# Converting float64 weights to float32 on the chip: the sign as whole words by PoolE, the low bits over it by ScalarE

## The chip, the cores and the metric

The kernel runs on one core of one Trainium2 chip. The core has five engines with queues of their own: TensorE (PE in the profile, with its weight loads as PEld), VectorE (DVE), ScalarE (ACT), PoolE (POOL) and SyncE (SP), which here issues the transfers. Each engine takes its instructions strictly in the order of its queue, and an instruction waits for those of other engines that it depends on. The metric is the device time of one execution in microseconds.

## The reference

Three layers stand one behind the other: a chunked state space layer ("attention"), a leaky MLP, and a mixture of experts with one expert per token.

```python
# x (4, 8, 768, 32), a (4, 8, 768), B and C (4, 8, 768, 16), float32, in chunks of 32
M = (C_c @ B_c.T) * exp(cum_i - cum_j) * causal
y = M @ x_c + (C_c @ state) * exp(cum)
state = exp(sum la) * state + sum_j B_j x_j exp(cum_last - cum_j)
# then rows of 256, 3072 tokens
h = x @ w_in                          # w_in (256, 2048), float64
x = (maximum(0.01 * h, h) @ w_out).astype(float32)   # w_out (2048, 256), float64
# then per token one of 8 experts, chosen by argmax of x @ w_gate + modality_bias
out[mask] = gate_w * (maximum(x[mask] @ w1[e], 0) @ w2[e])
```

The inputs w_in and w_out come as float64, since they are float32 arrays divided by a float64 number. [...]

## The kernel before

The tokens go through in blocks of 512. For a block, four attention chunks of 128 tokens are computed (attn_tr or attn_split and attn_stack, attn_cb, attn_p3), and their result xh, xl (the float32 value as a rounded part and a rest, both of type float32r) is multiplied by w_in in 16 column tiles (mm1, which makes h, then sa, gg, gh, gl) and by w_out (mm2, which sums into y). Six matmuls per pair of tiles do the work of one product of float32 accuracy: each weight, too, is a rounded part (wih, woh) and a rest (wil, wol).

The weights are converted in the first part of the program, 16 tiles of 128x512 numbers, eight of w_in (split_win, two per column quarter) and eight of w_out (split_wout). Each lies in SBUF as raw (four 16-bit words per number) and goes through to_f32, in five steps on three engines, and then two of split:

- ACT writes hb from the high word of the float64 (as a float32 it has 8 exponent bits, the scale of 2^-112 moves the exponent into place).
- POOL writes the two 16-bit halves of the word lb: into the lower half a number worked out from the second 16-bit word of raw (times LOW plus LOW0, the "low" operation), into the upper half the sign (the fourth 16-bit word of raw is_ge 32768, times 32768, the "sign" operation).
- DVE shifts hb left by 3 and ors lb over it.
- ACT rounds hb into wih or woh (split, s.copy), and POOL subtracts that from hb into wil or wol (split, eng is POOL for all tiles, by Q['sg']).

hb and lb have two buffers each (the tags "hb" and "lb" of pool ap_): hb of a tile can be written only when the subtraction of the tile two before is done, and lb only when DVE's or of the tile two before is done. POOL also masks e, the decay of an attention chunk (attn_mask, the affine select), after its transfer from cumd has landed. The first four tiles (buffers 292, 350, 547 and 555) are converted in the prologue, the other twelve while block 0 is multiplied: mm1 of column tiles 4 to 7 needs the tiles 605 and 631, and so on in order.

A scheduler that simulates a timeline sets the order of the instructions on each engine from the order in which the program lists them. Where the table Q['pin'] names a function, the operations of the engines that it gives stay in the program's order. keep (the matmuls wps of zeros) is there to keep TensorE busy.

Of the kernel before, what the change touches and what calls it, by code (L numbers as in the profile page):

```python
# [13 lines left out]
AF = mybir.ActivationFunctionType  # L14
ALU = mybir.AluOpType
# [5 lines left out]
LOW, LOW0 = 0.9 * 2.0 ** -13, 0.2995  # L21
# [68 lines left out]
def kernel(  # L90
# [70 lines left out]
    v, s, g, t_ = Pinned(nc.vector, "v"), Pinned(nc.scalar, "s"), Pinned(nc.gpsimd, "g"), Pinned(nc.tensor, "t")  # L161
# [375 lines left out]
    def to_f32(raw, q):  # L537

        w = raw.bitcast(I32).rearrange("p (f w) -> p f w", w=2)
        hb = ap_.tile([P, 512], F32, tag="hb", name="hb")  # L540
        lb = ap_.tile([P, 512], I32, tag="lb", name="lb")
        s.activation(out=hb, in_=w[:, :, 1].bitcast(F32), func=AF.Copy, scale=2.0 ** -112)
        w4 = raw.bitcast(U16).rearrange("p (f w) -> p f w", w=4)
        l2 = lb.bitcast(U16).rearrange("p (f w) -> p f w", w=2)
        g.tensor_scalar(out=l2[:, :, 0], in0=w4[:, :, 1], scalar1=LOW, scalar2=LOW0, op0=ALU.mult, op1=ALU.add)
        g.tensor_scalar(out=l2[:, :, 1], in0=w4[:, :, 3], scalar1=32768.0, scalar2=32768.0, op0=ALU.is_ge, op1=ALU.mult)
        hi = hb.bitcast(I32)
        v.scalar_tensor_tensor(out=hi, in0=hi, scalar=3, in1=lb, op0=ALU.logical_shift_left, op1=ALU.bitwise_or)
        return hb
# [13 lines left out]
    def split_win(k, kk):  # L563
        r = raws["i", k]
        os = slice(k * 512, (k + 1) * 512)
        f = to_f32(r[:, kk, :], kk) if W64 else r[:, kk, :]
        split(f, wih[:, kk, os], wil[:, kk, os], g if kk in Q["sg"] else v)
# [6 lines left out]
    def split_wout(k, q):  # L574
        r = raws["o", k]
        os = slice(k * 4 + 2 * q, k * 4 + 2 * q + 2)
        f = r[:, 2 * q:2 * q + 2, :].rearrange("p a d -> p (a d)")
        f = to_f32(f, q) if W64 else f
        split(
            f, woh[:, os, :].rearrange("p a d -> p (a d)"), wol[:, os, :].rearrange("p a d -> p (a d)"), g if q in Q["sg"] else v  # L580
        )
# [485 lines left out]
```

## Time and profile before

| | us |
|---|---|
| runs, median of 3 (lowest, highest) | 571.35 (570.81, 574.28) |
| the profiled execution, own time | 569.56 |
| its span, first to last instruction | 567.7 |
| busy in the span: PE, DVE, ACT, POOL | 529.3, 355.7, 332.7, 213.7 |
| mean granted TensorE clock | 0.962 |

The profiled execution has 1.86 us around its span and lies 1.79 us below the median of the runs. In the names of the trace buffer numbers are left out; in the orders of the program they stand, so lb_695 and hb_694 are the same tile's buffers. Every instruction has line 154, that of a helper that records them, so instructions are told apart by the names of their tiles: the line tells nothing. A bracket at the end of a timeline row is the idle time of the engine before it, and what released it.

### The profile page before, as it was taken

Reading aid. Unit: us, or ns where it says so; the run is one execution under the profiler, and the core shown is the slowest. Engines: PE = TensorE matmul, PEld = TensorE weight load, DVE = VectorE, ACT = ScalarE, POOL = GpSimd, SP = SyncE. Lnnn points to the kernel's source line nnn. Section 1 sums busy time; section 2 is a strip of 40 time slices with the busy share of each in tenths; the row PEclk is TensorE's granted clock in tenths of the full one; section 3 lists DMA queues with packets and bytes.
Section 4 is the critical chain, followed back from the end, with each engine's and each line's share of the span. In section 5 each row is a group of like instructions: output and inputs, shape, how many; then the busy total and the mean of one; then the engine's idle time right before and its main releaser. Section 6 shows DMA issues by size and latency. Waiting matters only on the chain.

```text
span 567.7 us, 9531 instructions
## 1 busy us (share of the span) xinstructions
PE 529.3 (93%) x3414; PEld 427.5 (75%) x3417; DVE 355.7 (63%) x707; ACT 332.7 (59%) x694; POOL 213.7 (38%) x184
## 2 busy tenths in 40 slices
PE   7888899699999999999999999999989999999990
PEld 3345465377876778878777787788879999999990
DVE  5646385787757676778576866656486566455630
ACT  4326566667676657775775675464436666566630
POOL 5838999810300120011200202431063445665431
PEclk9978888999999999999999999999979999999996
DMA  7897442232133315421322084412054765777400
GB/s 141 178 211 177 124 161 51 57 61 57 9 90 75 79 12 94 103 57 13 71 72 47 2 149 134 149 38 75 1 167 136 242 201 188 235 236 239 129 20 23
DMA packets 128440, 61.13 MB, mean 108 GB/s; under 512 B 84641, under 2 KB 120642, under 8 KB 128386
## 3 DMA queue, kind: packets, MB, share of 16 engines
q1 hardware_dynamic: 125314, 54.03, 37.6%
q0 software_dynamic: 3072, 6.42, 3.4%
q8 instruction: 29, 0.48, 0.4%
q14 instruction: 25, 0.20, 0.1%
HBM read 53.74 MB, written 6.69 MB: 106 GB/s over the span
## 4 chain that ended last, share of the span: by engine, by line
PE 75%; POOL 7%; issue 6%; DVE 5%; ACT 3%; DMA 1%; SPq 1%; POOLq 0%; DVEq 0%
PE h L154 21%; PE y L154 20%; PE hp L154 11%; PE o L154 10%; PE psy L154 5%; POOL lb L154 3%; PE cb L154 2%; POOL e L154 1%; PE yr L154 1%; PE pb L154 1%; PE xps L154 1%; PE pc L154 1%; DVE gl L154 1%; PE lp L154 1%; DVE hb L154 1%
## 5 line engine op out<-in xcount | busy, mean ns | idle before, releaser
L154 DVE TENSOR_TENSOR gl<-gg,gh 128x512 fp32r<-128x512 f32 x96 | 71.4, 744 | 44.6 <-ACT gh L154 44.0
L154 ACT CAST gh<-gg 128x512 fp32r<-128x512 f32 x96 | 59.5, 620 | 67.9 <-DVE gg L154 67.8
L154 PE MATMUL h<-xh,wih 128*128 128x512 f32 x192 | 79.0, 416 | 5.5 <-DVE gg L154 5.1
L154 DVE TENSOR_TENSOR gg<-sa,h 128x512 f32<-128x512 f32 x96 | 65.5, 682 | 23.2 <-ACT sa L154 22.8
L154 POOL TENSOR_SCALAR_AFFINE_SELECT e<-e 128x1024 f32<-128x1024 f32 (+1 forms) x28 | 28.9, 1044 | 134.0 <-DMA e<-cumd 70.2
L154 PE MATMUL h<-xh,wil 128*128 128x512 f32 x192 | 77.0, 403 | 2.0 <-POOL wil L154 1.9
L154 PE MATMUL h<-xl,wih 128*128 128x512 f32 x192 | 77.0, 401 | 1.4 <-DVE xl L154 1.4
L154 PE MATMUL y<-gl,woh 128*128 128x512 f32 x192 | 77.3, 406 | 0.7 <-DVE gl L154 0.7
L154 PE MATMUL y<-gh,wol 128*128 128x512 f32 x192 | 75.2, 397 | 1.2 <-POOL wol L154 1.2
L154 PE MATMUL hp<-x2h,w1s 128*128 128x256 f32 x384 | 73.9, 288 | 0.0
L154 ACT ACTIVATE sa<-h 128x512 f32<-128x512 f32 x96 | 57.3, 597 | 22.5 <-PE h L154 22.2
L154 PE MATMUL o<-w2s,hh 128*128 128x256 f32 x384 | 69.2, 285 | 0.0
L154 DVE SCALAR_TENSOR_TENSOR hl<-hp,hh 128x512 fp32r<-128x512 f32 x48 | 33.0, 691 | 54.9 <-ACT hh L154 54.8
L154 PE MATMUL y<-gh,woh 128*128 128x512 f32 x192 | 65.9, 407 | 0.0
L154 POOL TENSOR_TENSOR w2s<-r,w2s 128x1024 fp32r<-128x1024 f32 x12 | 33.5, 2792 | 79.8 <-ACT w2s L154 53.8
L154 PEld LDWEIGHTS hp<-x2h,w1s 128*128 128x128 f32 x384 | 62.9, 197 | 0.6
L154 PEld LDWEIGHTS o<-w2s,hh 128*128 128x128 f32 x384 | 58.3, 191 | 0.4 <-issue 0.4
L154 POOL TENSOR_SCALAR lb<-raw 128x512 uint16<-128x512 uint16 x32 | 51.3, 1602 | 14.5 <-issue 11.7
L154 PE MATMUL hp<-x2l,w1s 128*128 128x256 f32 x192 | 54.6, 289 | 0.0
L154 ACT ACTIVATE hh<-hp 128x512 fp32r<-128x512 f32 x48 | 28.5, 597 | 41.9 <-PE hp L154 41.9
L154 PE MATMUL o<-w2s,hl 128*128 128x256 f32 x192 | 51.1, 283 | 0.0
L154 ACT ACTIVATE e<-e,ncum 128x128 f32<-128x128 f32 x160 | 50.9, 392 | 0.0
(205 smaller groups left out, 997.8 us busy)
## 6 DMA issues: line engine op xcount, KB each, us to landing
r<-in_moe_w_dram SPq DMA_DIRECT2D x48, 512.0 KB, 4.5
e<-cumd SPq DMA_DIRECT2D x20, 512.0 KB, 4.7
raw<-in_moe_w_in_dram SPq DMA_DIRECT2D x4, 1024.0 KB, 6.7
raw<-in_moe_w_out_dram SPq DMA_DIRECT2D x4, 1024.0 KB, 5.8
yx<-ysb SPq DMA_DIRECT2D x6, 528.0 KB, 3.6
xt<-in_x_dram SPq DMA_DIRECT2D x24, 128.0 KB, 4.3
ct<-in_C_dram SPq DMA_DIRECT2D x24, 64.0 KB, 3.1
bt<-in_B_dram SPq DMA_DIRECT2D x24, 64.0 KB, 2.7
```

The source lines that it names most:

```text
L154: r = f(*args, **kw)
```

## The change

The sign operation of POOL writes a whole 32-bit word now (-2^31 or 0, as int32) instead of its upper half, and the low operation moves from POOL to ACT, which writes the lower half of the same word with an activation (Copy with a scale and a bias). What is computed for lb is the same. ACT's write has to follow POOL's, and DVE's or waits for ACT's instead of POOL's.

```diff
@@ to_f32
         s.activation(out=hb, in_=w[:, :, 1].bitcast(F32), func=AF.Copy, scale=2.0 ** -112)
         w4 = raw.bitcast(U16).rearrange("p (f w) -> p f w", w=4)
         l2 = lb.bitcast(U16).rearrange("p (f w) -> p f w", w=2)
-        g.tensor_scalar(out=l2[:, :, 0], in0=w4[:, :, 1], scalar1=LOW, scalar2=LOW0, op0=ALU.mult, op1=ALU.add)
-        g.tensor_scalar(out=l2[:, :, 1], in0=w4[:, :, 3], scalar1=32768.0, scalar2=32768.0, op0=ALU.is_ge, op1=ALU.mult)
+        g.tensor_scalar(out=lb, in0=w4[:, :, 3], scalar1=32768.0, scalar2=-(2.0 ** 31), op0=ALU.is_ge, op1=ALU.mult)
+        s.activation(out=l2[:, :, 0], in_=w4[:, :, 1], func=AF.Copy, scale=LOW, bias=LOW0)
         hi = hb.bitcast(I32)
         v.scalar_tensor_tensor(out=hi, in0=hi, scalar=3, in1=lb, op0=ALU.logical_shift_left, op1=ALU.bitwise_or)
```

The scheduler makes a new order of it. On POOL, in the program before, this stands from the first conversion after the four masks of chunks 4 to 7 on (lb are the sign and low operations, wil and wol the subtractions, e_913 is the mask of chunk 8):

```order
L154 TENSOR_SCALAR lb_695<-raw_194 128x512 x2
L154 TENSOR_TENSOR wil_141<-hb_605,wih_140 128x512
L154 TENSOR_SCALAR lb_744<-raw_194 128x512 x2
L154 TENSOR_TENSOR wil_141<-hb_631,wih_140 128x512
L154 TENSOR_SCALAR lb_752<-raw_639 128x512 x2
L154 TENSOR_TENSOR wol_143<-hb_694,woh_142 128x512
L154 AFFINE_SELECT e_913<-e_913 128x1024
L154 TENSOR_SCALAR lb_781<-raw_639 128x512 x2
L154 TENSOR_TENSOR wol_143<-hb_743,woh_142 128x512
```

And in the changed program, at the same place on POOL:

```order
L154 TENSOR_SCALAR lb_695<-raw_194 128x512
L154 TENSOR_TENSOR wil_141<-hb_605,wih_140 128x512
L154 TENSOR_SCALAR lb_744<-raw_194 128x512
L154 TENSOR_TENSOR wil_141<-hb_631,wih_140 128x512
L154 TENSOR_SCALAR lb_752<-raw_639 128x512
L154 TENSOR_TENSOR wol_143<-hb_694,woh_142 128x512
L154 AFFINE_SELECT e_913<-e_913 128x1024
L154 TENSOR_SCALAR lb_781<-raw_639 128x512
L154 TENSOR_TENSOR wol_143<-hb_743,woh_142 128x512
```

POOL's order is kept, with one operation per tile in place of two; the sign of a tile stands one subtraction ahead of that of the tile two before it.

On ACT, before, from the conversion of the first tile of the second column quarter on (btt and cdt belong to attention chunks, e are the exponentials of the masked decay, sa is the first step behind mm1):

```order
L154 ACTIVATE hb_605<-raw_192 128x512
L154 COPY btt_823<-ps_818 128x128
L154 ACTIVATE hb_631<-raw_192 128x512
L154 CAST wih_140<-hb_605 128x512
L154 CAST wih_140<-hb_631 128x512
L154 ACTIVATE e_534<-e_534,ncum_122 128x128 x8
L154 ACTIVATE e_542<-e_542,ncum_122 128x128 x4
L154 ACTIVATE cdt_826<-ps_818,mask2_107 128x128 x2
L154 ACTIVATE hb_694<-raw_194 128x512
L154 CAST woh_142<-hb_694 128x512
```

And on ACT in the changed program:

```order
L154 ACTIVATE hb_605<-raw_192 128x512
L154 ACTIVATE lb_606<-raw_192 128x512
L154 ACTIVATE hb_631<-raw_192 128x512
L154 ACTIVATE lb_632<-raw_192 128x512
L154 CAST wih_140<-hb_605 128x512
L154 CAST wih_140<-hb_631 128x512
L154 ACTIVATE e_534<-e_534,ncum_122 128x128 x8
L154 ACTIVATE e_542<-e_542,ncum_122 128x128 x4
L154 COPY btt_823<-ps_818 128x128
L154 ACTIVATE lb_695<-raw_194 128x512
L154 ACTIVATE cdt_826<-ps_818,mask2_107 128x128 x2
L154 ACTIVATE hb_694<-raw_194 128x512
```

Each tile has one more activation, lb. For the tiles of w_in (606, 632 and, further on, 752, 781, 940, 948) it stands behind hb of its tile; for those of w_out (695 here, then 744, 851, 892, 1016, 1048) ahead of it. On DVE the ors of these tiles keep their order among each other, and the or of hb_547 and hb_555 keeps its place in the queue. Behind the conversions the scheduler also orders the products h and y of the later blocks differently in places; the instructions are the same ones.

## Rows read from the trace of the kernel before

**Rows 1.** The page: span, busy time by engine, the chain that ended last.
```profile
span 567.7 us, 9531 instructions
...
PE 75%; POOL 7%; issue 6%; DVE 5%; ACT 3%; DMA 1%; SPq 1%; POOLq 0%; DVEq 0%
```
**Rows 2.** Busy time by stretch (start:end, length, engines, PEclk granted, DMA share, GB/s).
```profile
core 0: us, PE busy (x) PEld busy (x) DVE busy (x) ACT busy (x) POOL busy (x), PEclk, DMA share, GB/s
44.50:114.00 69.50, 58.37 (x240) 36.61 (x239) 43.39 (x65) 42.76 (x102) 65.61 (x45) 0.89 0.45 115
115.00:520.00 405.00, 399.66 (x2671) 338.93 (x2670) 270.20 (x554) 253.74 (x528) 107.36 (x85) 0.99 0.38 102
```
**Rows 3.** POOL in order of time, 44.5 to 114 us.
```profile
44.52 7.08 POOL L154 TENSOR_SCALAR lb<-raw 128x512 uint16<-128x512 uint16 x4 [11.75 <-issue]
...
59.25 3.04 POOL L154 TENSOR_SCALAR lb<-raw 128x512 uint16<-128x512 uint16 x2
62.24 1.25 POOL L154 TENSOR_TENSOR wil<-hb,wih 128x512 fp32r<-128x512 f32 x1
...
72.31 1.55 POOL L154 TENSOR_SCALAR_AFFINE_SELECT e<-e 128x1024 f32<-128x1024 f32 x1
74.50 2.97 POOL L154 TENSOR_SCALAR lb<-raw 128x512 uint16<-128x512 uint16 x2 [0.63 <-DVE hb L154]
...
111.62 1.10 POOL L154 TENSOR_SCALAR_AFFINE_SELECT e<-e 128x1024 f32<-128x1024 f32 x1 [1.68 <-DVE hb L154]
112.68 1.46 POOL L154 TENSOR_TENSOR wol<-hb,woh 128x512 fp32r<-128x512 f32 x1
```
**Rows 4.** The chain that ended last, from 59 us on (start, us, what).
```profile
60.18 2.11 POOL lb L154
62.29 1.21 POOL wil L154
63.55 2.54 PE h L154 x6
```
**Rows 5.** POOL's conversions by group, 44.4 to 114.2 us (busy, mean ns).
```profile
L154 POOL TENSOR_SCALAR lb<-raw 128x512 uint16<-128x512 uint16 x24 | 39.3, 1637 | 13.9 <-issue 11.7 <-DVE hb L154 0.6
```
**Rows 6.** Operations on tile lb near 14, 44.5, 60.2 and 104.9 us (min/median/max ns).
```profile
L154 POOL TENSOR_SCALAR lb<-raw x2: 765/1442/2120, 14.0 to 14.8; 128x512 uint16<-128x512 uint16 x2
...
L154 POOL TENSOR_SCALAR lb<-raw x1: 1896/1896/1896, 44.5 to 44.5; 128x512 uint16<-128x512 uint16 x1
...
L154 POOL TENSOR_SCALAR lb<-raw x1: 2111/2111/2111, 60.2 to 60.2; 128x512 uint16<-128x512 uint16 x1
...
L154 POOL TENSOR_SCALAR lb<-raw x1: 2621/2621/2621, 104.9 to 104.9; 128x512 uint16<-128x512 uint16 x1
```
**Rows 7.** Operations on tile hb, whole span (min/median/max ns).
```profile
L154 ACT ACTIVATE hb<-raw x16: 651/674/723, 13.0 to 109.2; 128x512 f32<-128x512 f32 x16
L154 DVE SCALAR_TENSOR_TENSOR hb<-hb,lb x16: 668/692/1578, 17.0 to 110.9; 128x512 int32<-128x512 int32 x16
L154 ACT CAST wih<-hb x8: 600/618/622, 17.7 to 101.7; 128x512 fp32r<-128x512 f32 x8
L154 POOL TENSOR_TENSOR wil<-hb,wih x8: 1252/1264/1274, 18.4 to 107.4; 128x512 fp32r<-128x512 f32 x8
```
**Rows 8.** ACT's groups, 44.4 to 114.2 us: hb and what it waited for.
```profile
L154 ACT ACTIVATE hb<-raw 128x512 f32<-128x512 f32 x12 | 8.1, 672 | 9.2 <-POOL wil L154 5.6 <-POOL wol L154 3.6
```
**Rows 9.** SP's issue of the decay of chunk 8, and the page's time to landing.
```profile
67.25 0.37 SPq L373 DMA_DIRECT2D e<-cumd  x1
...
e<-cumd SPq DMA_DIRECT2D x20, 512.0 KB, 4.7
```
**Rows 10.** PE and DVE in order of time before 44.5 us.
```profile
29.29 0.47 PE L154 MATMUL ps<-ident,bt 128*128 128x128 f32 x1 [0.89 <-DMA bt<-in_B_dram]
...
33.73 1.49 PE L154 MATMUL wps<-zer 128*128 128x512 bf16 x3 [0.33 <-issue]
...
43.70 1.27 DVE L154 SCALAR_TENSOR_TENSOR hb<-hb,lb 128x512 int32<-128x512 int32 x2
```
**Rows 11.** DVE while POOL ran a subtraction and the mask of 72.31 us.
```profile
71.46 1.45 DVE L154 TENSOR_TENSOR gl<-gg,gh 128x512 fp32r<-128x512 f32 x1 [0.69 <-ACT gh L154]
72.83 1.58 DVE L154 SCALAR_TENSOR_TENSOR hb<-hb,lb 128x512 int32<-128x512 int32 x1
```

## The prediction

> **What bounds the kernel now.** I read the page first, for the chain that ended last: PE holds 75% of it and POOL 7% [rows 1], and POOL's part needs a place. The busy times by stretch give it: from 115 to 520 us PE is busy 399.66 of 405 us at a clock of 0.99, so there PE sets the pace and nothing that POOL does can matter; from 44.5 to 114 us PE is busy 58.37 of 69.5 us at a clock of 0.89, and POOL 65.61 of 69.5 [rows 2]. That is the stretch in which the last twelve weight tiles are converted. POOL's timeline shows that it hardly ever waits in it: 0.63 and 1.68 us, and the last subtraction starts at 112.68 [rows 3]. The chain shows who waits: POOL's lb, then its wil, then the products h that need wil [rows 4]. So from 44.5 to 114 us POOL is the bound, and what is taken from it there is gained, as far as another engine doesn't become late: PE's work in the stretch is worth 58.37 x 0.89 = 52 us at full clock, ACT's 42.8 and DVE's 43.4 us [rows 2].
>
> **The low operation leaves POOL.** One tile's two operations were 765 and 2120 ns in the quiet pair at 14 us [rows 6]. The low operation stands first in the program and so is the 765; the sign operation, which stays, is the dear one. In the stretch, twelve pairs took 39.3 us [rows 5], 3.27 us a pair. The sign operation took 2.11 us when alone and 2.62 when disturbed [rows 6]; with their middle, 2.33, a pair leaves 0.94 us for the low operation (it, too, is at times disturbed, 1.90 us at 44.5 us [rows 6]). Twelve times 0.94 is **11.3 us** off POOL. With 2.11 it is 13.9 us, with 2.62 7.8 us: these ends stay in the range.
>
> **The sign operation in its new form.** It writes int32 words side by side instead of every second half word, and multiplies by another number. The trace has no such operation. The nearest row is the old one, 2.11 to 2.62 us, with the same input and the same two operators, so I take it unchanged. From below, 0.77 us bounds it (the other operation on the same shapes); from above nothing in the trace does, and the rival on that takes a dearer one.
>
> What disturbs POOL shows on DVE's side: gl took 1.45 us and the or 1.58, where an undisturbed or takes 0.69 [rows 7, 11], both operations with two inputs in SBUF. The Trainium skill (SBUF — State Buffer, "Who interferes with whom") says that VectorE with two SBUF inputs and PoolE share a read port by an exclusive lock, and that the second to come blocks until the first has finished. By that rule each sign operation could pay a whole or, 2.11 + 0.69 = 2.80 us, and the relief would be 39.3 - 12 x 2.80 = 5.7 us instead of 11.3. The rows show less, +0.51 us at most for the sign operation, so the rows' 2.33 stands.
>
> **The low operation comes to ACT.** Twelve activations of the cost of hb, 674 ns, with the same stride over raw [rows 7]: 8.1 us. That makes 42.8 + 8.1 = 50.9 us of ACT work, for a stretch that POOL alone would shorten to 69.5 - 11.3 = 58.2 us: ACT would be busy 87% of it. Each activation lies on the way from POOL's sign to DVE's or. Behind a waiting one the queue holds sa and gh of mm1, the exponentials e and the casts, so DVE's gg and PE's h would wait for it. By the order, six of the twelve (w_out) stand ahead of hb of their tile. There ACT waited for POOL's subtraction, 9.2 us in all [rows 8], and the sign was done before that subtraction; these six are hidden in that wait. The other six (w_in) stand between hb and the or, 6 x 0.67 = 4.0 us. Their cover is POOL's own work: while hb, low and or run (0.67 + 0.67 + 0.69 = 2.03 us [rows 7]), POOL does the next tile's sign and a subtraction, 2.33 + 1.26 = 3.6 us. The slack of 1.6 us is half of what it was before (3.27 + 1.26 = 4.5 us of POOL work over hb and or, 1.37 us, so 3.2 us), and even that was used up twice, by 0.63 and 1.68 us more [rows 3]. I take half of the 4.0 us as lost, **2.0 us**; the ends are 0 and all 8.1 us.
>
> **The mask that comes too early.** The mask of chunk 8 ran at 72.31 with no wait [rows 3]. Its transfer was issued at 67.25 and takes 4.7 us [rows 9], until 71.95; the issue follows products that stand behind the h of 63.55 [rows 4], which waited for the third tile's turn on POOL. That h comes 3 x 0.94 = 2.8 us earlier, so the transfer lands at 69.1; POOL arrives five tiles, 4.7 us, earlier, at 67.6. POOL waits **1.5 us** there. The loads of raw follow the conversions that free their buffers and move forward with them.
>
> **Nothing before 44.5 us.** Four tiles are converted there. For the first two the low operation leaves the way to the or on POOL (0.77 us) and comes back on ACT (0.67). The masks of chunk 3 come about 3 us earlier, but PE waits for the transfer of bt until 29.29 us and has products and the filling wps in front of that chunk [rows 10]. The other two tiles end in the ors at 43.70 [rows 10], which stand in DVE's queue behind work that follows PE; POOL starts again at 44.52 only when the first or has freed lb [rows 3]. If that cover were gone, it would be a gain of 0.8 us a tile at most; I take 0.
>
> **The sum.** 11.3 - 2.0 - 1.5 = 7.8 us off the stretch. It becomes 61.7 us, above PE's 52 and ACT's 50.9, so neither is the bound by its work alone. From 115 us on, PE-bound work follows earlier by as much, and the tail with it. 569.56 - 7.8 = 561.8 us for an execution like the profiled one; the median of the runs is 1.79 us above that one, so **563.5 us**.
>
> **Rivals.** *The sign gets cheap as well.* If the whole-word form costs 0.77 us like the other operation, POOL loses another 12 x 1.56 = 18.7 us, and the bound becomes PE and ACT, 52 and 51 us, in an order that lets neither be full; with 57 us for the stretch the gain is 12.5 us and the time **559 us**. For it: two operations of one shape differ by 1.35 us [rows 6], so something in the old form is slow that shape doesn't explain. Against: the slow one keeps its operators. The Trainium skill (GPSIMD Engine Reference, "3.1 Elementwise — side-by-side cycle accounting") gives 768 ns as the price of 512 elements in a tight loop without data-dependent branches; the 765 ns row agrees, and the sign's 2.1 us doesn't.
>
> *ACT takes POOL's place.* If all 8.1 us of the activations and the 1.5 us of the mask are lost, 1.7 us of gain is left: **569.5 us**. For it: 87% busy in a queue that waits in order; against: half of the activations stand where ACT waited anyway.
>
> *The sign gets dearer: slower than before.* The place is POOL, 12 signs in the stretch. It decides from 7.8 / 12 = 0.65 us more per sign, 3.0 us instead of 2.33. If the conversion to int32 costs as much again as the two old operations differ, 1.35 us, the stretch gets 16.2 us longer, 8.4 net: **580 us**. Against: POOL's other operations that write 32-bit words aren't slow for that (wil 1.26 us with two inputs [rows 7]).
>
> **How the numbers follow.** About 1%, 5.7 us, is what can be told from no change here. The forecast has 0.50, with a range of its own of 561 to 567 us (relief of 7.8 to 13.9 less 3.5). The cheap sign has 0.13, ACT in POOL's place 0.25, the dear sign 0.08; 0.04 is for a new order of the later products that costs or gives 1 to 4 us. Faster by over 1% is below 565.6 us: 0.42 of the forecast's 0.50, the cheap sign, and a little of the third, 0.58. Slower by over 1%: the dear sign and half of the last, 0.10. The rest, 0.32, is no change. The range, 557.5 to 571.5 us, takes in the first three cases and leaves out the dear sign and the ends of the others.
>
> **What would show it.** In the changed kernel's profile POOL has 16 operations lb of type int32 with means of 2.1 to 2.6 us, and ACT 16 activations lb of about 0.67 us. The conversions restart at 44.5 us as before; the first subtraction after the four masks comes about 2.8 us before 62.24; a wait for a transfer of about 1.5 us stands before the mask of chunk 8; the last subtraction starts near 105 instead of 112.68 us; and POOL waits more often for DVE hb than the two times. PE's busy time from there on is the same. The prediction is wrong if lb on POOL isn't near 2.3 us, if ACT's sa and gh start later after their h and gg than before by more than the 2.0 us in sum, or if the gain at 112 us is given back before the end.

## The result, and the profile after

The changed kernel takes 564.71 us (median of 4 runs, 563.16 to 565.19) beside 572.82 us of the kernel before (4 runs, 570.81 to 574.55): a ratio of 0.9855, with an interval of 0.981 to 0.99. Six further runs beside another set of the kernel before gave 562.31 and 573.26 us, ratio 0.9797 (0.9751 to 0.9842). So the change gains 8 to 11 us; 7.8 was forecast, and 563.5 us. Of all runs below, two of one kernel (g_no_low, 567.5 and 567.6 us, at a lower clock than its others) were slow ones and are left out of its figures.

The page of the changed kernel, span and chain that ended last, beside [rows 1]:

```profile
span 563.0 us, 9533 instructions
...
PE 71%; ACT 7%; DVE 6%; issue 3%; POOL 1%; POOLq 0%; DVEq 0%; ACTq 0%
```

POOL's share of the chain went from 7% to 1%, ACT's from 3% to 7%. Busy time by stretch of the changed kernel (columns as in [rows 2]):

```profile
44.50:114.00 69.50, 60.58 (x266) 38.45 (x265) 44.76 (x72) 50.55 (x116) 51.28 (x33) 0.90 0.45 115
```

POOL is busy 51.28 us there instead of 65.61, ACT 50.55 instead of 42.76, and PE got 266 matmuls done instead of 240. The conversions by group (busy, mean ns | idle before), POOL, ACT and DVE, 44.4 to 114 us:

```profile
L154 POOL TENSOR_SCALAR lb<-raw 128x512 int32<-128x512 uint16 x12 | 25.2, 2104 | 17.7 <-ACT gh L154 14.0 <-DVE hb L154 3.7
...
L154 ACT ACTIVATE lb<-raw 128x512 uint16<-128x512 uint16 x12 | 9.4, 779 | 0.0
...
L154 DVE SCALAR_TENSOR_TENSOR hb<-hb,lb 128x512 int32<-128x512 int32 x12 | 11.0, 922 | 9.1 <-ACT lb L154 5.8 <-ACT hb L154 3.3
```

POOL's 39.3 us [rows 5] are 25.2 now; the low operation costs ACT 9.4 us. DVE's or waits for ACT's lb now. The same three operations over the whole span (min/median/max ns), beside [rows 6, 7]:

```profile
L154 POOL TENSOR_SCALAR lb<-raw x16: 1947/1969/3098, 15.0 to 98.4; 128x512 int32<-128x512 uint16 x16
L154 ACT ACTIVATE lb<-raw x16: 757/780/812, 17.0 to 102.8; 128x512 uint16<-128x512 uint16 x16
L154 DVE SCALAR_TENSOR_TENSOR hb<-hb,lb x16: 622/692/1757, 17.8 to 104.7; 128x512 int32<-128x512 int32 x16
```

POOL's timeline of the changed kernel, beside [rows 3]:

```profile
43.94 5.05 POOL L154 TENSOR_SCALAR lb<-raw 128x512 int32<-128x512 uint16 x2 [14.04 <-ACT gh L154]
...
58.96 1.26 POOL L154 TENSOR_TENSOR wil<-hb,wih 128x512 fp32r<-128x512 f32 x1
...
65.50 1.97 POOL L154 TENSOR_SCALAR lb<-raw 128x512 int32<-128x512 uint16 x1 [2.08 <-DVE hb L154]
...
71.71 1.10 POOL L154 TENSOR_SCALAR_AFFINE_SELECT e<-e 128x1024 f32<-128x1024 f32 x1 [2.99 <-DVE hb L154]
...
84.63 1.97 POOL L154 TENSOR_SCALAR lb<-raw 128x512 int32<-128x512 uint16 x1 [1.59 <-DVE hb L154]
88.07 1.29 POOL L154 TENSOR_TENSOR wol<-hb,woh 128x512 fp32r<-128x512 f32 x1 [1.47 <-ACT woh L154]
...
94.14 1.10 POOL L154 TENSOR_SCALAR_AFFINE_SELECT e<-e 128x1024 f32<-128x1024 f32 x1 [1.56 <-DMA e<-cumd]
...
102.99 1.28 POOL L154 TENSOR_TENSOR wol<-hb,woh 128x512 fp32r<-128x512 f32 x1 [1.28 <-ACT woh L154]
107.64 1.25 POOL L154 TENSOR_SCALAR_AFFINE_SELECT e<-e 128x1024 f32<-128x1024 f32 x1 [3.38 <-DVE c L154]
108.87 1.26 POOL L154 TENSOR_TENSOR wol<-hb,woh 128x512 fp32r<-128x512 f32 x1
```

The first subtraction behind the masks comes 3.3 us earlier than before (58.96, 62.24), but the last only 3.8 us (108.87, 112.68). Between them POOL waits seven times, 14.35 us in all (12.4 in the second trace of the changed kernel), where it waited 2.31 us before. What the change took from POOL it mostly spends waiting. Who made it wait shows in the chain that ended last, cut to 44.5 to 114 us; first the kernel before, then the changed one (shares of that stretch by engine and tile):

```profile
by line: issue 30.4%; POOL lb L154 18.4%; PE h L154 11.1%; POOL e L154 6.4%; DVE gl L154 5.7%; DMA e<-cumd 5.5%; POOL wol L154 5.4%; PE psy L154 5.4%; DVE hb L154 4.7%; PE cb L154 4.7%; DVE gg L154 3.7%; POOL wil L154 3.6%; ACT gh L154 2.7%
```

```profile
by line: ACT e L154 9.7%; issue 7.3%; DVE gl L154 7.2%; DVE hb L154 7.2%; PE h L154 4.9%; ACT lb L154 4.2%; ACT gh L154 4.1%; DVE gg L154 3.8%; ACT woh L154 3.2%; PE y L154 3.0%; POOL lb L154 2.8%; ACT wih L154 2.5%; ACT hb L154 2.4%; ACT s
...
57.27 3.01 ACT e L154 x10
...
64.13 0.57 ACT hb L154
64.72 0.70 DVE hb L154
65.45 0.62 ACT woh L154
66.07 1.18 ACT e L154 x4
67.25 0.67 ACT lb L154
67.91 0.51 ACT hb L154
68.42 0.56 ACT sa L154
69.01 0.70 DVE gg L154
69.73 0.63 ACT gh L154
70.39 0.69 DVE gl L154
71.08 0.61 DVE hb L154
```

Before, POOL's operations on lb, e, wol and wil hold 33.8% of the stretch. Afterwards no engine holds it. The chain, which can be followed back to 56 us in this trace, goes to and fro between ACT and DVE, mostly in steps of 0.5 to 0.7 us, with the steps of the conversion (hb, or, woh, lb) and those of mm1 (sa, gg, gh, gl) mixed in the same two queues. In the second trace of the changed kernel PE's h has 12.8% of it, DVE's or 10.4% and ACT's e 8.0%, and POOL's lb 2.8% again.

### The profile page after: what moved, and what is told of

The parts are those of the page before. It is cut to its first block, busy times and chain, and to the rows that moved or that the text cites. A ratio compares the mean times of both kernels' runs of the same rounds, so it can differ in the third digit from the quotient of the medians.

```text
span 563.0 us, 9533 instructions
## 1 busy us (share of the span) xinstructions
PE 525.6 (93%) x3414; PEld 426.0 (76%) x3417; DVE 352.8 (63%) x707; ACT 341.4 (61%) x710; POOL 197.1 (35%) x168
## 3 DMA queue, kind: packets, MB, share of 16 engines
q1 hardware_dynamic: 125314, 54.03, 38.1%
## 4 chain that ended last, share of the span: by engine, by line
PE 71%; ACT 7%; DVE 6%; issue 3%; POOL 1%; POOLq 0%; DVEq 0%; ACTq 0%
PE h L154 20%; PE y L154 19%; PE hp L154 11%; PE o L154 10%; PE psy L154 4%; PE cb L154 2%; ACT e L154 2%; DVE gl L154 1%; ACT gh L154 1%; PE pb L154 1%; PE pc L154 1%; PE yr L154 1%; DVE hb L154 1%; DVE gg L154 1%; PE xps L154 1%
## 5 line engine op out<-in xcount | busy, mean ns | idle before, releaser
L154 POOL DMA_INDIRECT il<-ids,pi x24 | 26.3, 1096 | 62.8 <-DVE pi L154 30.9
```

Source lines behind the costliest of these rows:

```text
L154: r = f(*args, **kw)
```

## The experiments

All kernels ran beside runs of the kernel before on the same chip; a ratio is to those, and a gain or loss in us is between the two medians. "Low" and "sign" are the two operations on lb, and "the logits" are those of block 0's gate, lt, which follow its last product.

**The kernel before, once more.**

> The kernel before once more, unchanged, to learn how far its runs and its profiled execution differ: the profiled execution took 569.56 us, the four timed runs 570.81 to 574.55. If 569.56 was a favourable execution, a new one lies at 571 to 574.5 us, and the gain of the change between typical executions is some 8 us, of which the two traces so far show 4.9. If 569.56 is typical for a profiled execution, this one lies within 569 to 570.5 and the timed runs are longer for a reason outside the trace.

572.19 us (567.17 to 574.28), ratio 1.0007 (0.9978 to 1.0036). The profiled execution took 568.52, one of the fastest of twelve, as the first profiled one (569.56) lay below its median.

**Is POOL the bound before?** The low operation done twice on POOL:

```diff
         g.tensor_scalar(out=l2[:, :, 0], ..., op0=ALU.mult, op1=ALU.add)
+        g.tensor_scalar(out=l2[:, :, 0], ..., op0=ALU.mult, op1=ALU.add)
```

> The kernel before with its low operation on POOL issued twice per tile (same result, written twice). My theory, POOL is the bound from 44.5 to 113 us in the kernel before: 12 x 0.84 to 0.94 us is added in full, 583 to 584 us (1.018 to 1.02). Rival, POOL has hidden slack there and the gain of the change came from elsewhere: 573 to 576 us.

582.9 us, ratio 1.0199 (1.0164 to 1.0234), +11.4 us. POOL's conversions by group (44.4 to 131 us), its restart and its last subtraction:

```profile
L154 POOL TENSOR_SCALAR lb<-raw 128x512 uint16<-128x512 uint16 x36 | 50.2, 1393 | 17.3 <-DVE hb L154 14.5
...
50.85 8.04 POOL L154 TENSOR_SCALAR lb<-raw 128x512 uint16<-128x512 uint16 x5 [14.52 <-DVE hb L154]
...
129.83 1.47 POOL L154 TENSOR_TENSOR wol<-hb,woh 128x512 fp32r<-128x512 f32 x1 [0.30 <-ACT woh L154]
```

The 12 further operations are 50.2 - 39.3 = 10.9 us. From POOL's restart to its last subtraction it now takes 78.98 us instead of 68.16, 10.8 more: inside the stretch all of the added work counts. That the time grows by nearly as much is in part chance. POOL restarts 6.3 us later (50.85, 44.52) behind a stretch, 30 to 44.5 us, in which PE's granted clock was 0.50 instead of 0.77; the logits come 16.6 us later (148.4, where the two traces of before have 131.2 and 132.4), and some of that is made up behind them. The other way round, every second subtraction moved to DVE, with the conversion as before:

```diff
-Q = {'sg': (0, 1),
+Q = {'sg': (0,),
```

> The kernel before with the subtractions of every second tile (eight in all, six behind 44 us) on VectorE instead of PoolE, and nothing changed in the conversion: 6 x 1.26 = 7.6 us less PoolE work between 44 and 113 us. If PoolE's work is the bound there, as the run with a doubled low operation says, and relief of any kind is given back one for one, 564 to 566 us beside 572. If relief brings more than its own work, because TensorE then waits less and its granted clock dips less, 560 to 563 us. If the gain of the changed kernel came from the new order of the later products and not from PoolE, 570 to 573 us, since this one has the order of before or another by accident.

562.32 us, ratio 0.9817 (0.9786 to 0.9849): 10.9 us less. Busy times, POOL's groups, its restart and its last subtraction:

```profile
44.50:114.00 69.50, 59.45 (x271) 37.67 (x271) 54.36 (x89) 47.05 (x113) 59.41 (x38) 0.98 0.47 117
...
L154 POOL TENSOR_SCALAR lb<-raw 128x512 uint16<-128x512 uint16 x24 | 41.1, 1713 | 14.2 <-issue 12.6
...
L154 POOL TENSOR_TENSOR wol<-hb,woh 128x512 fp32r<-128x512 f32 x4 | 5.5, 1386 | 0.0
L154 POOL TENSOR_TENSOR wil<-hb,wih 128x512 fp32r<-128x512 f32 x3 | 4.4, 1460 | 0.0
...
45.70 7.82 POOL L154 TENSOR_SCALAR lb<-raw 128x512 uint16<-128x512 uint16 x4 [12.57 <-issue]
...
103.79 1.27 POOL L154 TENSOR_TENSOR wol<-hb,woh 128x512 fp32r<-128x512 f32 x1
```

The kernel before has 14 subtractions on POOL in the stretch, 18.4 us (the groups of 10.8 and 7.6 us below). Seven are left, 9.9 us; that is 8.5 us less and not the 7.6 that were expected, while lb takes 1.8 us more.

```profile
L154 POOL TENSOR_TENSOR wol<-hb,woh 128x512 fp32r<-128x512 f32 x8 | 10.8, 1359 | 0.0
...
L154 POOL TENSOR_TENSOR wil<-hb,wih 128x512 fp32r<-128x512 f32 x6 | 7.6, 1260 | 0.0
```

The last subtraction comes 8.9 us earlier (103.79, 112.68), and the granted clock of the stretch is 0.98 instead of 0.89. So relief of POOL of another kind, with no operation of the change in it, is worth as much as the change. In both runs POOL hardly waits between its restart and its last subtraction (0.30 us with low doubled, not at all here), and the time between them follows POOL's work up and down, 78.98, 68.16 and 58.09 us: POOL was the bound. The gain of 10.9 us is more than the 6.7 that POOL was relieved of on balance; the new order of later products (below) and the clock may have a part in it, and no run separates them.

**The two halves of the change.** First the sign as whole words, with low still on POOL behind it:

```diff
-        g.tensor_scalar(out=l2[:, :, 0], ..., op0=ALU.mult, op1=ALU.add)
-        g.tensor_scalar(out=l2[:, :, 1], ..., scalar2=32768.0, ...)
+        g.tensor_scalar(out=lb, ..., scalar2=-(2.0 ** 31), ...)
+        g.tensor_scalar(out=l2[:, :, 0], ..., op0=ALU.mult, op1=ALU.add)
```

> One part alone: the sign as whole words (1.97 us where the half words took 2.11 to 2.62), the low operation still on POOL, behind it. My theory: POOL stays the bound from 44.5 to 113 us and is relieved by 12 x 0.14 to 0.36 us, 1.7 to 4.3 us: 568.5 to 571 us, 0 to 0.7% below before. Rival, the word form alone makes the gain: 564 to 566 us. Rival, only the new order of later products makes it: 572.8 us, no change.

566.58 us, ratio 0.991 (0.9881 to 0.9939): more than expected, for 2.3 us less on lb (37.0 instead of 39.3). In its trace block 0's logits aren't earlier than before (lt at 133.4; before 131.2 and 132.4); the gain lies behind them, where its products stand in another order, as they do in all but one of the edited kernels (see below). Then low on ACT, and the sign as half words (b_low_act):

```diff
-        g.tensor_scalar(out=lb, ..., scalar2=-(2.0 ** 31), ...)
+        g.tensor_scalar(out=l2[:, :, 1], ..., scalar2=32768.0, ...)
         s.activation(out=l2[:, :, 0], ...)
```

> The other part alone: the low operation by ACT, the sign still as upper half words by POOL (2.11 us alone). My theory: the low operation's leaving POOL is what gives the gain; POOL is relieved of 11.3 us less the same give-back on ACT as in the changed kernel, 565 to 567.5 us. Rival, the word form makes the gain: 570 to 573 us. Rival, POOL is still the bound in the changed kernel: the half words' 12 x 0.14 to 0.36 us are lost in full, 566.5 to 569 us.

559.77 us, ratio 0.9794 (0.9762 to 0.9825): below every range that was expected of it, and 5 us below the changed kernel's first four runs. Half words don't overlap, so here ACT's low waits for no sign. I took that for the cause: in the changed kernel sign, low and or stand in series over three engines. Three runs tested it. In one, low of b_low_act is made to wait for the sign (i_b_wait):

```diff
+        tc.add_manual_dep(low.ins, sign.ins.name, ..., reason="the sign first")
```

> The half-word sign on PoolE and the low operation on ScalarE, as in b_low_act (559.77 us, before at 571.5), but each low activation has to wait for its tile's sign, as the overlap of the two writes makes it do in the changed kernel. My theory: the changed kernel loses its 5 us against b_low_act by this wait (PoolE's sign, then ScalarE's low, then VectorE's or, in series), so this one comes out at 564 to 567 us. Rival: the loss lies in the whole-word operation itself or in nothing but an accident of the order; then it stays at 559 to 561 us.

561.05 us, ratio 0.9807 (0.9779 to 0.9835). And both kernels again, side by side:

> The changed kernel unchanged, in more runs. i_b_wait has its order of instructions nearly to the end and differs by the half-word sign; it came out at 561.05 us (ratio 0.9807), where four runs of the changed kernel gave 564.71 (0.9855, interval 0.981 to 0.99). If the whole-word form itself costs something, this stays at 564 to 566 us. If the four runs lay high by chance, 561 to 563 us.

> b_low_act again (559.77 us), on the same chip as after_again. If the wait of ScalarE's low for PoolE's sign costs the changed kernel something, b_again stays 3 us or more below after_again; if it is only 1 to 2 us, as i_b_wait says, 559.5 to 560.5 us beside 561 to 562 us there.

562.31 us, 0.9797 (0.9751 to 0.9842), for the changed kernel, and 563.12 us, 0.9817 (0.9772 to 0.9862), for the other. That theory falls: the 5 us between the first two were a matter of few runs, and the wait costs nothing that these runs can tell. Half words and whole words can't be told apart either.

**Does ACT cost anything?** The changed kernel with low done twice on ACT, and with low left out (then the low three bits of the weights are missing):

```diff
         s.activation(out=l2[:, :, 0], ...)
+        s.activation(out=l2[:, :, 0], ...)
```

> The changed kernel with each low activation on ScalarE done twice: 12 x 0.78 = 9.4 us more ScalarE work in the stretch, 16 x 0.78 in all. If ScalarE's queue has become the bound (the rival that ScalarE takes PoolE's place), all of it shows: 573 to 575 us. By my theory it is the serial way over sign, low and or, and it counts for the six tiles on which VectorE waited for ScalarE: 6 x 0.78 = 4.7 us, 568 to 571 us. If ScalarE's work is hidden, 564 to 566 us.

562.1 us, ratio 0.9837 (0.9801 to 0.9872): 9.3 us more on ACT, and no loss. Busy times and ACT's group:

```profile
44.50:114.00 69.50, 57.00 (x261) 35.59 (x260) 49.42 (x74) 57.97 (x126) 50.64 (x33) 0.98 0.44 115
...
L154 ACT ACTIVATE lb<-raw 128x512 uint16<-128x512 uint16 x24 | 18.7, 778 | 0.0
```

ACT is busy 57.97 of 69.5 us there, and the logits come at 127.5 us (127.9 and 126.5 in the two traces of the changed kernel). PE's clock in the stretch was 0.98 where the changed kernel's was 0.90 and 0.93, so a cost of a few us may be hidden by that.

> The changed kernel without the low operation on any engine (the low three bits of every weight are left out): PoolE's relief alone, with nothing given to ScalarE. By the prediction's step (2.0 us lost on ScalarE) 2 us below after_again; by the run that did the low operation on ScalarE twice (562.1 us, no loss) within 1 us of it; if the way over sign, low and or in series costs 5 us, 5 us below it, 557 to 560 us.

559.57 us (four runs, 558.1 to 564.11), ratio 0.9776 (0.9715 to 0.9836), 2.7 us below the changed kernel on the same chip. The profiled execution, the fastest, has block 0's logits at 122.5 us, 4 us before the changed kernel's. But the runs spread too far to tell a gain of 2 us from none, and this kernel differs in one thing more.

**The order behind block 0.** Edits around the conversion make the scheduler order the later products anew, and the traces show which order ran. PE's second group of yr (the transposes of a finished block) starts when 174 products h are done in the kernel before and in g_no_low, and when 162 are done in every other kernel here: the relief of POOL (l_before_sub) and the doubled low (c_before_plus), too, have the changed kernel's order and not that of before. So they don't separate POOL's work from the order, but g_no_low does: with the order of before and POOL relieved, it gains as much as the changed kernel. The order by itself is worth little. From the logits to the end of the span the three traces with the old one take 436.5, 434.3 and 433.8 us and the eleven with the new one 431.0 to 435.1, 433.0 on average: some 2 us, and two executions of b_low_act (431.0 and 434.0) differ by as much.

**Is POOL still a bound after?** The changed kernel with a further low on POOL, between the sign and ACT's:

```diff
         g.tensor_scalar(out=lb, ...)
+        g.tensor_scalar(out=l2[:, :, 0], ..., op0=ALU.mult, op1=ALU.add)
         s.activation(out=l2[:, :, 0], ...)
```

> The changed kernel with one more low operation per tile on PoolE, behind the sign and ahead of ScalarE's, which writes over it: 12 x 0.8 to 0.9 us = 9.6 to 11 us more PoolE work between 44 and 108 us, where PoolE waited 14.5 us in the trace of the changed kernel. If PoolE is still the bound there, 574 to 576 us. By my theory PoolE isn't the bound by its work any more, and what counts is the way from the sign over ScalarE to the or, on which VectorE waited for six of the twelve tiles: 6 x 0.8 = 4.8 us, 568 to 571 us. If the added work is wholly hidden in PoolE's waits, 564 to 565 us.

567.54 us, ratio 0.9925 (0.989 to 0.996), a gain of 5.0 us where the changed kernel has 8.1 and 11.0: 35.9 - 25.2 = 10.7 us more on POOL cost 3 to 6 us, and the logits come 6 to 7.5 us later (134.0), where the kernel before paid its 10.9 in full. And b_low_act with every second subtraction on DVE:

> b_low_act (559.8 us) with the subtractions of every second tile (eight in all, six behind 44 us) on VectorE instead of PoolE: 6 x 1.26 = 7.6 us less PoolE work in the stretch, as much or a little less more on VectorE. If PoolE is still the bound in b_low_act, 554 to 557 us. If TensorE and ScalarE have taken over, 559 to 561 us. If VectorE's or and gl come late behind the subtractions, 562 us or more.

553.65 us (551.42 to 554.78), ratio 0.9657 (0.9631 to 0.9683), the fastest of all: it gains 18.9 us, b_low_act 11.8 and 10.1. Busy times:

```profile
44.50:114.00 69.50, 61.42 (x307) 39.92 (x307) 55.90 (x90) 55.44 (x130) 46.86 (x27) 1.00 0.50 125
```

PE does 307 matmuls in the stretch, and its granted clock is 1.00. So POOL's steps still lie on the way after the change, though POOL isn't full any more; whether by POOL's time or by what its subtractions do to DVE (next section) isn't separated.

## Why the prediction was right, point by point

**The bound** was named rightly: 10.9 us more on POOL made its stretch 10.8 us longer, 6.7 us less on balance made it 10.1 us shorter (one mask fell behind its end), and the relief of POOL with the old order of products (g_no_low) gained as much as the change.

**The relief** was 39.3 - 25.2 = 14.1 us, where 11.3 stood in the sum. With half words it is 39.3 - 26.2 = 13.1 (26.2 is the same group in b_low_act), so a low operation cost 1.09 us in the stretch and not 0.94; the sign's new form gives the other 1.0. The sign took 2.10 us on average (1.97 in the median) against 2.33: neither the cheap sign (0.77) nor the dear one (3.0 and more) came. The rule of the Trainium skill (SBUF — State Buffer, "Who interferes with whom"), by which each sign might wait out a whole or and the relief be 5.7, isn't borne out for the sign: one of 16 signs took 3.10 us, the median is 1.97, and the half-word sign of b_low_act, the form of the kernel before, took 26.2 / 12 = 2.18 us on average. DVE's operation doesn't wait there either: the or at 73.68 took its 0.69 us while the sign of 72.78 to 74.74 ran. For POOL's subtractions the trace agrees with the rule, and it is DVE that comes second:

```profile
73.68 0.69 DVE L154 SCALAR_TENSOR_TENSOR hb<-hb,lb 128x512 int32<-128x512 int32 x1 [1.40 <-ACT lb L154]
...
78.19 1.77 DVE L154 TENSOR_TENSOR gl<-gg,gh 128x512 fp32r<-128x512 f32 x1
...
100.50 1.76 DVE L154 SCALAR_TENSOR_TENSOR hb<-hb,lb 128x512 int32<-128x512 int32 x1
```

POOL's subtractions beside the last two end at 79.41 and 101.70, and DVE's operations end 0.55 us behind them. Both stand on the chain that ended last, so part of what keeps the stretch long is DVE behind POOL's subtractions, a term that the sum doesn't have.

**Low on ACT** took 780 ns and not the 674 of hb, 9.4 us and not 8.1. The 2.0 us put down as lost stay open: doubling it loses nothing, leaving it out gains 2.7 us in the medians, within the spread of the runs. One sign that the prediction named against itself did come. Over block 0's 16 column tiles sa starts 47.7 and 46.8 us in sum behind its h in the two traces of the changed kernel (counting six products h to a tile in order of time), 38.1 and 36.8 before: 10 us more, where 2.0 was the limit. It is 35.0 with low left out and 53.0 with low twice, so it follows low on ACT; but the time doesn't follow it, and gh behind gg is no later (5.7 in both, 4.4 and 5.9 before). The rival that ACT takes POOL's place is refuted as a matter of ACT's work; on the chain ACT's share did rise.

**The mask** of chunk 8 waited 2.99 us and not 1.5. The trace names DVE's or, which ended just then. But SyncE's row of the changed kernel puts the issue of the transfer at 67.07:

```profile
67.07 0.37 SPq L373 DMA_DIRECT2D e<-cumd  x1
```

With the 4.7 us of [rows 9] it would have landed at 71.77, and the mask starts at 71.71, so the transfer may have held it as well. The step that failed is that the issue would come 2.8 us earlier: it came 0.2 us earlier. That the products ahead of it follow ACT's and DVE's steps by then is what the chain suggests; no run tests it. The next mask, at 94.14, waited 1.56 us for its transfer.

**Before 44.5 us** little moved, as said: POOL restarts at 43.94 and 44.48 in the two traces instead of 44.52.

**The step that was mis-sized** is the sum over the stretch: "what is taken from it there is gained, as far as another engine doesn't become late". Three terms, 11.3 - 2.0 - 1.5, made 7.8 us; of 14.1 us POOL gave 12 back in waits (10 in the second trace), and the last subtraction came at 108.87 and 107.45 instead of near 105. In the traces the gain up to block 0's logits is 3.3 to 5.9 us (lt at 127.9 and 126.5 in the two traces of the changed kernel, 131.2 and 132.4 in those of before), and 5.6 at the end (mean span 561.65 against 567.2). I looked for a single engine with more work than 61.7 us and found none, rightly; but a path over ACT, DVE, PE and POOL, each with gaps, was what came next. The gain wasn't given back behind 112 us: from the logits to the end both kernels take the same time within 3 us.

**The offset.** I added 1.79 us, by which the profiled execution lay under the median of before. Both profiled executions of before lie low among their runs; those of the changed kernel don't (564.70 beside 564.71, 562.04 beside 562.31). So the gain in medians, 8.1 and 11.0 us, is larger than the 5.6 of the traces, and the forecast of 563.5 came out well partly because two errors, 2.2 us too much in the stretch and 1.8 too much in the offset, go against each other. What the executions differ in is the granted clock: 0.950 to 0.967 in the runs of the kernel before, 0.964 to 0.974 in the ten of the changed one. As an estimate, PE's 529.3 us at 0.962 are 509 us of full-clock work; they take 531 us at 0.959 and 524 at 0.971. Runs in which PE waits less for POOL tend to show higher clocks in the stretch (0.81 with low doubled, 0.88 and 0.89 before, 0.90 and 0.93 in the changed kernel, 0.98 and 1.00 with the subtractions on DVE), so part of the gain is probably given by the clock and not by POOL's time itself; no run sets the clock by itself, and that share stays open. So does the gain of the whole-word sign alone: from logits to end the two traces of before take 436.5 and 434.3 us, its own 431.3, the changed kernel's 435.1 and 433.8, and executions of one kernel differ by as much.

## What to carry to other kernels

Where one engine is busy 94% of a stretch and hardly waits, as POOL was here, work added there counted in full, and what was taken away paid until a path of dependent steps over several engines took over; look for that path in the chain cut to the stretch, not only for the next engine by its busy time. Test a bound from both sides, by doubling an operation of it and by relieving it in a way that has nothing to do with the change: here every second subtraction on DVE, one number in a table, gave as much as the change, and together with low on ACT 19 us. Where a scheduler sets the order, compare the orders that ran as well: nearly every edit here brought the same new order of the later products with it, and only one run relieved POOL without it. Few runs don't tell two kernels 5 us apart: the ratios of four and six runs, 0.981 to 0.99 and 0.9762 to 0.9825, overlapped from the start, a theory was built on their difference, and it fell with six more of each.

## What the runs showed of the hardware that was not expected

The sign costs 1.95 to 1.97 us on POOL as 512 whole words and 2.09 to 2.12 as half words, while low, with the same input stride, costs 0.77 when undisturbed: that points at the operators (is_ge and mult, where low has mult and add), and not at the stride or width of what is written, as the dear part. The compare is the likely one, though no run has it by itself. ACT's lb, 16-bit in and out at a stride, takes 780 ns where hb, 32-bit at a stride, takes 674.

POOL's subtraction holds up an or or gl of DVE that begins beside it: in the changed kernel's stretch four of them took 1.27 to 1.77 us instead of 0.69. POOL's sign doesn't: the eight that began beside one took at most 0.69.

PE's granted clock differs between two executions of the same program at the same place. In the changed kernel from 8 to 12 us, first profile and then the second:

```profile
8.00:12.00 4.00, 4.00 (x23) 2.32 (x21) 1.76 (x5) 2.29 (x5) 0.54 (x1) 0.63 1.04 275
```

```profile
8.00:12.00 4.00, 3.69 (x31) 2.32 (x30) 2.57 (x7) 2.37 (x6) 1.23 (x2) 1.00 1.00 250
```

With 0.63 (mostly the lower level, 1.2 GHz) PE got 23 matmuls done where it did 31 at full clock, and everything behind stood about 1 us later: one more reason not to read a microsecond out of two traces.
